# Two reorderings on the tensor engine in batch 0 of an attention and gated-MLP kernel

## The chip, the cores and the metric

The kernel runs on one core of one Trainium2 chip; runs are compared within a job where it can be done. The metric is the device time of one execution in microseconds (us). Engines are written as in the profile: PE is the tensor engine (matmuls), PEld its weight loads, DVE the vector engine, ACT the scalar engine, POOL the GpSimd engine, which issues the loads. In the lines of the profile, 64*128 or 128*128 behind a matmul is the part of the array that it uses, the chain is the sequence of work that ended last, followed back from the end, and "issue" is idle time for which the profile shows no cause.

## The reference

```python
B, H, S, Nb, D = 8, 8, 576, 16, 64
k_all = concatenate([beacon_k, k]);  v_all = concatenate([beacon_v, v])     # 592 keys
scores = q @ k_all.T / sqrt(D), future keys masked with -1e9
a = exp(scores - max);  a /= a.sum() + 1e-9
x = (a @ v_all) as [4608, 512]
# ... [cut: types]
out = (gelu(x @ w_gate) * (x @ w_val)) @ w_out                             # 512 -> 1536 -> 512
```

## The kernel before

Heads are worked in four pairs (0 to 3) per batch. Scores of a pair come in chunks (pair, chunk): matmuls with 64 rows of K, two heads side by side on the two halves of the array, each chunk followed by one exp on ACT. Three PSUM buffers of the pool `psum_s` go round between score chunks, values pairs and gates; `psum_t` and `psum_o` hold one buffer each. In batch 0 the causal mask is added on PE by small matmuls with an identity.

```python
def scores(b, *parts):
    s_ps = psum_s.tile([P, 2, 512], FP32, name="s_ps", tag="s")     # one of three
    # ... score_mms: 64-row matmuls, then the masking matmuls
    act(exp_ring[...], s_ps[...], ACT.Exp, scale=QK_SCALE)
def av(b, m):                       # values of both heads: 30 matmuls, in psum_s
    # ... attend, attend, normalize (reciprocal and product on DVE)
def av_head(b, m, hi, pool, tag):   # one head: 15 matmuls, in psum_t or psum_o
    # ...
def turn(b, m, pool=None, tag="t"): # five PE transposes of the normalised pair
    # ...
def put(b, m, by_act=False):        # copies the turned pair to xT_sb on ACT or DVE
    # ...
```

The order of batch 0's second half, with `c` for `scores(0, ...)`:

```python
c((3, 0)); c((3, 2))
av_head(0, 0, 0, psum_t, "t"); av_head(0, 0, 1, psum_o, "o")
c((2, 3), (3, 3)); av(0, 1); c((3, 1)); av(0, 2)
turn(0, 0); put(0, 0, by_act=True); turn(0, 1, psum_o, "o"); put(0, 1, by_act=True)
av(0, 3); gv_mms(0, 0, 0); turn(0, 2); put(0, 2, by_act=True)
# ... [cut: table load]
gv_mms(0, 1, 0); turn(0, 3, psum_o, "o"); put(0, 3)
for kk in (1, 2, 3):
    for fi in (0, 1):
        gv_mms(0, fi, kk, last=kk == 3)        # gate and value matmuls of row chunk kk
```

The softmax here doesn't subtract the row's maximum and nothing guards it: scores larger than these inputs give would overflow.

## Time and profile before

| what | before |
|---|---|
| time, median of the first three runs | 365.41 us (364.52 to 365.82) |
| profiled span | 363.6 us |
| PE busy | 353.7 us, 97% |
| first weights of (3,0), released by DVE's key copy | 15.87 us |
| first weights of the last turn | 23.71 us |

The prediction shows the lines of the page, the chain of waits and the timeline. The columns are start, length, engine, line, operation, operands and count; in brackets is the idle time before and what ended it.

```profile
19.20 0.11 PEld L168 LDWEIGHTS <-qkT 64*128 64x128 bf16 x4
19.60 0.11 PEld L168 LDWEIGHTS <-eye 64*128 64x128 bf16 x3 [0.29 <-issue]
```

Four weight loads come together at 19.20, and then PE's stream stands for 0.29 us with nothing to wait for that the profile knows ("issue").

### The profile page before, as it was taken

The numbers are of one execution on the slowest core, as the hardware profiler recorded it, in microseconds if no ns is written. First come the engines' busy times: TensorE is split into PE (matmuls) and PEld (weight loads), VectorE is DVE, ScalarE is ACT, GpSimd is POOL, SyncE is SP. The second block draws the span as 40 slices with busy tenths as digits, with TensorE's granted clock in tenths as the row PEclk, the third lists the DMA queues.
The fourth block names the chain that finished last, engine by engine and source line by source line (L and its number), as shares of the span: only waits on it lengthen the run. The fifth ranks groups of instructions, "written<-read, shape, count | busy, mean of one in ns | idle before, by whom it ended". The sixth has DMA issues, their size and how long they took to land.

```text
span 363.6 us, 7732 instructions
## 1 busy us (share of the span) xinstructions
PE 353.7 (97%) x3164; PEld 187.5 (52%) x3206; DVE 163.4 (45%) x320; ACT 193.0 (53%) x252; POOL 161.3 (44%) x288
## 2 busy tenths in 40 slices
PE   7899999999999999999999999999999999999996
PEld 7664546444654455445644564446544554444443
DVE  3548746344453345434534354335443453333322
ACT  3975788237923694358633891379335953321210
POOL 8934387556536552945374545565330530000000
PEclk9999999999999999999999999999999999999999
DMA  8999999899289975999299927993795142000112
GB/s 112 174 203 204 196 121 97 125 156 199 30 128 135 215 58 71 168 217 62 56 138 205 138 38 122 162 198 35 111 147 127 15 65 113 0 2 29 58 38 108
DMA packets 160419, 41.57 MB, mean 114 GB/s; under 512 B 146944, under 2 KB 155904, under 8 KB 160384
## 3 DMA queue, kind: packets, MB, share of 16 engines
q0 software_dynamic: 104848, 19.11, 68.4%
q1 hardware_dynamic: 55536, 21.96, 30.9%
q8 instruction: 25, 0.41, 0.5%
q14 instruction: 10, 0.08, 0.1%
HBM read 38.27 MB, written 9.44 MB: 131 GB/s over the span
## 4 chain that ended last, share of the span: by engine, by line
PE 88%; DMA 5%; DVE 3%; POOL 2%; issue 1%; ACT 0%; SPq 0%; POOLq 0%
PE gv_ps L168 40%; PE o_ps L168 25%; PE x_ps L168 9%; PE s_ps L168 6%; DMA q_sb<-in_q_dram 3%; PE v_ps L168 3%; PE g_ps L168 3%; PE t_ps L176 2%; DMA k_sb<-in_k_dram 1%; DVE qkT L235 1%; POOL v_sb L111 1%; PE w_ps L168 1%; DVE o_sb L481 1%; DMA xT_sb<-y_sb 1%; POOL k_sb L111 0%
## 5 line engine op out<-in xcount | busy, mean ns | idle before, releaser
L171 ACT ACTIVATE ge_sb<-gv_ps 128x512 bf16<-128x512 f32 x95 | 55.8, 597 | 134.7 <-PE gv_ps L168 132.4
L433 DVE TENSOR_TENSOR hT_sb<-gv_ps,ge_sb 128x512 bf16<-128x512 f32 x95 | 64.9, 691 | 105.4 <-ACT ge_sb L171 105.3
L171 ACT ACTIVATE expT<-s_ps 128x992 bf16<-128x992 f32 (+3 forms) x112 | 100.5, 975 | 11.3 <-PE s_ps L168 9.8
L168 PE MATMUL gv_ps<-xT_sb,wg_sb 128*128 128x512 bf16 x378 | 105.1, 379 | 0.5
L168 PE MATMUL o_ps<-wo_sb,hT_sb 128*128 128x512 bf16 (+3 forms) x492 | 101.0, 373 | 2.3 <-DVE o_sb L481 0.9
L168 PE MATMUL gv_ps<-xT_sb,wv_sb 128*128 128x512 bf16 x364 | 101.7, 379 | 0.4
L320 POOL TENSOR_SCALAR_AFFINE_SELECT expT<-expT 128x256 bf16<-128x256 bf16 (+1 forms) x140 | 52.4, 391 | 48.4 <-ACT expT L171 47.1
L168 PEld LDWEIGHTS <-wv_sb 128*128 128x128 bf16 x432 | 42.2, 98 | 50.6
L168 PEld LDWEIGHTS <-wg_sb 128*128 128x128 bf16 x432 | 42.1, 98 | 49.9
L168 PEld LDWEIGHTS <-hT_sb 128*128 128x128 bf16 (+1 forms) x516 | 40.8, 96 | 43.8 <-issue 5.4
L168 PEld LDWEIGHTS <-expT 128*128 128x128 bf16 (+1 forms) x960 | 33.7, 97 | 9.0 <-POOL expT L320 3.1
L168 PE MATMUL x_ps<-v_sb,expT 128*128 128x65 bf16 (+1 forms) x960 | 36.8, 193 | 0.0
L111 POOL DMA_DIRECT2D v_sb<-in_v_dram x40 | 33.7, 861 | 6.1 <-DMA wv_sb<-in_moe_w_val_dram 2.4
L168 PE MATMUL s_ps<-qkT 64*128 64x80 bf16 (+5 forms) x528 | 33.1, 250 | 2.4 <-DVE qkT L239 1.6
L111 POOL DMA_DIRECT2D k_sb<-in_k_dram x30 | 25.2, 843 | 16.8 <-DMA v_sb<-in_v_dram 8.3
L111 POOL DMA_DIRECT2D q_sb<-in_q_dram x30 | 25.3, 874 | 9.9 <-DMA wo_sb<-in_moe_w_out_dram 3.6
L356 DVE TENSOR_TENSOR y_sb<-x_ps,r_sb 128x320 bf16<-128x320 f32 (+1 forms) x47 | 28.8, 612 | 1.8 <-DVE r_sb L354 0.2
L354 DVE RECIPROCAL r_sb<-x_ps 128x5 f32<-128x5 f32 (+1 forms) x47 | 9.6, 204 | 38.9 <-PE x_ps L168 38.9
L479 DVE COPY o_sb<-o_ps 128x512 f32<-128x512 f32 (+2 forms) x31 | 20.7, 668 | 13.3 <-PE o_ps L168 12.7
L168 PEld LDWEIGHTS <-qkT 64*128 64x128 bf16 x528 | 18.6, 95 | 14.0 <-issue 6.1
L399 POOL COPY hold_sb<-xT_sb 128x2 bf16<-128x2 bf16 x6 | 1.1, 186 | 31.9 <-DMA xT_sb<-y_sb 31.9
L433 DVE TENSOR_TENSOR hT_sb<-v_ps,ge_sb 128x512 bf16<-128x512 f32 x13 | 9.0, 692 | 9.5 <-PE v_ps L168 9.5
(58 smaller groups left out, 153.7 us busy)
## 6 DMA issues: line engine op xcount, KB each, us to landing
out_dram<-o_sb SPq DMA_DIRECT2D x35, 256.0 KB, 7.0
v_sb<-in_v_dram POOLq DMA_DIRECT2D x24, 128.0 KB, 9.2
q_sb<-in_q_dram POOLq DMA_DIRECT2D x18, 128.0 KB, 12.8
k_sb<-in_k_dram POOLq DMA_DIRECT2D x18, 128.0 KB, 5.5
wo_sb<-in_moe_w_out_dram POOLq DMA_DIRECT2D x3, 512.0 KB, 14.6
wg_sb<-in_moe_w_gate_dram POOLq DMA_DIRECT2D x2, 512.0 KB, 11.3
wv_sb<-in_moe_w_val_dram POOLq DMA_DIRECT2D x2, 512.0 KB, 13.1
v_sb<-in_v_dram POOLq DMA_DIRECT2D x8, 112.0 KB, 5.7
```

The lines of the kernel that those rows point to most:

```text
L111: keep(nc.gpsimd.dma_start(out=out_ap, in_=in_ap))
L168: keep(nc.tensor.matmul(out_ap, lhsT, rhs, start=start, stop=stop, **kw))
L171: keep(nc.scalar.activation(out_ap, in_ap, func, **kw))
L176: keep(nc.tensor.transpose(out_ap, in_ap, ident[0:n, 0:n]))
L235: keep(nc.vector.tensor_copy(out_ap, in_ap))
L320: nc.gpsimd.affine_select(out=d, in_=d, pattern=[[0, 2], [1, n]], compare_op=ALU.is_ge, fill=0.0, base=0, channel_multiplier=-1,)
L354: keep(nc.vector.reciprocal(r, x[:, :, :, D:DV]))
L356: nc.vector.tensor_tensor(out=y_of[i][:, :, h0:h1, :].rearrange("p j b d -> p b j d"), in0=x[:, :, :, 0:D], in1=r.to_broadcast([P, h1 - h0 ...
L399: keep(nc.gpsimd.tensor_copy(hold_sb, x[:, 0 : S : S - 1]))
L433: keep(nc.vector.tensor_tensor(out=h_of[ci][:, fi, :], in0=v_ps, in1=ge_sb, op=ALU.mult))
L479: keep(nc.vector.tensor_copy(o_ap, o_ps))
L481: keep(nc.vector.tensor_copy(o_ap, o_half))
```

## The change

The first values head of pair 0 is computed one score chunk sooner, while chunk (3,2)'s score buffer is not yet free. The turn of pair 0 goes ahead of values pair 2, so that its copy on ACT follows straight behind the last exp.

```diff
     c((3, 0))
+    av_head(0, 0, 0, psum_t, "t")
     c((3, 2))
-    av_head(0, 0, 0, psum_t, "t")
     av_head(0, 0, 1, psum_o, "o")
     c((2, 3), (3, 3))
     av(0, 1)
     c((3, 1))
+    turn(0, 0)
     av(0, 2)
-    turn(0, 0)
     put(0, 0, by_act=True)
```

## The prediction

> **What bounds the kernel now.** I read the page first (busy shares, then the chain that ended last), then that chain between 12 and 28 us only, and then the timeline of the tensor engine (PE), of its weight loads (PEld), of the scalar engine (ACT) and of the vector engine (DVE) from 14 to 25 us, because the diff touches nothing outside batch 0's values.
>
> ```profile
> PE 353.7 (97%) x3164; PEld 187.5 (52%) x3206; DVE 163.4 (45%) x320; ACT 193.0 (53%) x252; POOL 161.3 (44%) x288
> PE 88%; DMA 5%; DVE 3%; POOL 2%; issue 1%; ACT 0%; SPq 0%; POOLq 0%
> ```
>
> PE is busy for 353.7 of 363.6 us and is 88% of the chain: a change gains only what it takes off PE's sequence, or off a wait in which PE stands still. The chain around the change:
>
> ```profile
> 14.32 1.42 DVE qkT L235 x2
> 15.75 0.08 DVE qkT L239
> 15.83 0.05 issue
> 15.88 0.90 PE s_ps L168 x12
> 16.78 1.02 PE x_ps L168 x30
> ...
> 20.08 1.02 PE x_ps L168 x30
> 21.10 0.53 PE y_ps L176 x10
> 21.63 0.93 PE x_ps L168 x30
> 22.56 0.02 issue
> 22.58 0.23 DVE r_sb L354
> ```
>
> The columns are start, length and what. PE is released at 15.88 us by DVE's copy of the last key tile and from there the chain runs on PE alone, through scores, values and two turns, to the end of the last values pair at 22.56. So both moves lie inside one stretch that PE's own order bounds. Now the single waits in it (start, length, engine, what; in brackets idle time and who ended it):
>
> ```profile
> 16.13 0.28 PEld L168 LDWEIGHTS <-qkT 64*128 64x128 bf16 x2
> 16.32 0.37 PE L168 MATMUL s_ps<-qkT 64*128 64x464 bf16 x2
> 16.52 0.26 PE L168 MATMUL s_ps<-neg,eye 64*128 64x64 bf16 x4
> 16.71 1.09 PE L168 MATMUL x_ps<-v_sb,expT 128*128 128x65 bf16 x30
> 17.73 0.26 PE L168 MATMUL s_ps<-qkT 64*128 64x208 bf16 x2
> ...
> 20.12 1.00 ACT L171 ACTIVATE expT<-s_ps 128x992 bf16<-128x992 f32 x1 [0.45 <-PE s_ps L168]
> 21.40 1.19 ACT L171 ACTIVATE xT_sb<-y_ps 128x576 bf16<-128x576 bf16 x2 [0.28 <-PE y_ps L176]
> 23.28 0.65 ACT L171 ACTIVATE xT_sb<-y_ps 128x576 bf16<-128x576 bf16 x1 [0.69 <-PE y_ps L176]
> 23.71 0.28 PEld L176 LDWEIGHTS <-y_sb 128*128 128x128 bf16 x5 [0.54 <-DVE y_sb L356]
> ```
>
> The reader is to see three things. Score chunk (3,2) has its first weights at 16.13, but its matmul starts only at 16.32. ACT waits 0.28 us for the turned pair 0, the wait that the second move aims at. And the only long stop of PE's sequence after 15.88 is the last turn, which waits for the normalised fourth pair, not for anything that is moved.
>
> **What the Trainium skill says.** TensorEngine Tiling (Array Packing), Tiling Modes, Key Properties: changing the tiling mode, not just the tile, drains the TensorE. Scores run here as 64*128 tiles, values as 128*128, so each change between them should cost. The trace agrees: the four small masking matmuls before another score take 0.08 to 0.09 us to the next start (14.80 to 14.89, 17.83 to 17.91), but 0.19 and 0.18 us before values (16.52 to 16.71, 18.00 to 18.18): 0.10 us for scores to values. Thirty values matmuls take 0.92 to 0.93 us when a turn or a gate matmul, also 128*128, follows (20.01 to 20.94, 21.46 to 22.38), but 1.02 when a score follows (16.71 to 17.73, 18.18 to 19.20): 0.095 us for the way back. Perfetto Trace Analysis, Per-instruction lifecycle, Tensor Engine Instruction: the profiler estimates a matmul's end. I therefore work with starts throughout. TensorE: Matmul & The Clock Gate, Single matmul latency: (398 + N)/2.4 ns warm, which for N = 80 is 0.20 us (an estimate from that page); the exp at 20.12 follows the last masking matmul, start about 19.89, by 0.23 us, so it roughly agrees.
>
> **Part one, the first values head (15 matmuls) goes ahead of chunk (3,2).** No instruction is added or removed; the listing of the two programs' orders differs on PE alone, and each engine has the same number of rows.
> Removed: a wait. Chunk (3,2) needs the score buffer of (2,2), one of three, whose exp runs from 15.28 for 0.94 us, to 16.22. PE is through with (3,0) at about 16.10 + 0.09 = 16.19, and (3,2) starts at 16.32: 0.13 us of standing. In the new order the head fills it, being in another buffer: -0.13 us.
> Can the head start then? Its exps, pair 0's, are long over. The values land about 6 us after their issues, which start from 6.99 to about 10.5: the last at some 16.0 to 16.5, and the head needs the last tile in its fifteenth matmul only, at about 16.75. I take it as no wait.
> Added: scores and values alternate once more. Before: (3,0) (3,2) | head 0, head 1 | (2,3)(3,3). After: (3,0) | head 0 | (3,2) | head 1 | (2,3)(3,3). One more change in each direction is 0.10 + 0.095 = +0.195 us.
> Step by step: (3,0) done 16.19; head 0 from 16.29 with 15 x 0.031 = 0.46 to 16.75; (3,2) from 16.85 for 0.20 + 0.09 = 0.29 to 17.13; head 1 from 17.23 to 17.69; (2,3)(3,3) at 17.79, where it is 17.73 today. Sum +0.195 - 0.13 = **+0.06 us** on PE.
> Does the later (3,2), 0.5 us, starve ACT? Exp (3,0) starts at 16.98 and exp (3,2) about 17.9. The scores are ready at about 17.13 + 0.2 = 17.3: 0.6 us to spare, no cost. The head's normalisation comes 0.5 us earlier on DVE, which had been idle for 1.56 us there; nothing on PE waits for it: the next user of that result is the turn, three microseconds later.
>
> **Part two, turn (0,0) ahead of values pair 2.** The turn is five transposes in 0.26 us (ten from 20.94 to 21.46). Pair 0 is normalised at 18.23 + 0.49 = 18.72, so it can run at 20.0 without a wait. PE's sum up to the end of pair 3 stays: the same 2 x 30 values matmuls and 10 transposes, all 128*128, so no further mode change. 0.0 us on PE.
> What moves: the copy of pair 0 on ACT need not wait for the turn, only for the last exp, which ends at 21.12: it starts at about 21.15 to 21.2 instead of 21.40, and the second copy ends at about 22.4 instead of 22.59. The first gate matmul needs the first copy, which today ends at 22.05, and starts at 22.38 because PE comes free then; the second copy is first needed at 23.95. Both had over 0.3 us of slack already. ACT's gain of 0.2 us is off the path: worth 0.
> Given back: pair 2 ends 0.26 us later, and its normalised result goes from 22.21 to about 22.5 (with the 0.06 of part one). Turn (0,2) loads it at 22.60 today, at about 22.66 then: just in time, 0.1 us of slack left.
> The end of the stage is pair 3's end, plus reciprocal and product on DVE (22.58 to 23.66), plus the last turn at 23.71. All shift by the +0.06.
>
> **Sum.** 365.41 + 0.06 = 365.47; I write 365.45, since half of such a sum can vanish in rounding of the starts. From 24 us on PE runs without a break, so it is carried to the end unless the chain's DMA share (5%) takes it in.
>
> **Rivals.** (a) The mode change is cheaper for a short run, and the removed wait stands: -0.13 to 0 us, 365.3. For: only four places are measured. Against: all four agree within 0.02 us. (b) The transfers bite: if the last values tile lands later than estimated, head 0 now stops in front of (3,2), up to 0.3 us, 365.75; for it speaks the estimate's half microsecond of doubt, against it that today's head at 16.71 shows no stop. (c) Turn (0,2) becomes the stop: if DVE is 0.1 us later than worked out, PE waits some 0.1 us, but the last turn waits for DVE anyway (0.54 us on the loads' row), and DVE's product for pair 3 is only late if the one before is; 365.45 to 365.55. (d) The intent comes true, copies earlier mean gates earlier, worth the 0.28 us of ACT's wait: 365.15. Against it: PE, not the copies, sets the first gate's start.
>
> **Range and chances.** All of these lie between -0.3 and +0.35 us, 0.1% of the span, below the spread of the three runs before (364.52 to 365.82, 1.3 us). So the range is set by that spread: 364.6 to 366.2. 2% would be 7.3 us, nearly the whole 8.3 us from 15.88 to 24.16 in which the change lies: within 2% has 0.98, the rest split evenly.
>
> **What would show it right or wrong.** Right: 15 values matmuls start at about 16.3, (3,2) near 16.85, two more gaps of 0.1 us; chunk (2,3)(3,3) starts 0.06 us later counted from the end of DVE's key copy; ACT's first copy waits for the exp instead of the turn and starts 0.2 us sooner; the last turn still waits for DVE. Wrong: a stop inside head 0 (b), a stop before turn (0,2) (c), the last turn more than 0.1 us sooner from the key copy (a, d), or a difference of over 0.5 us that arises after 25 us, where no instruction moved.

## The result

| | before | changed |
|---|---|---|
| first comparison, median of 6 runs each | 365.51 us (364.52 to 365.82) | 365.02 us (364.92 to 365.40) |
| ratio, 95% interval | | 0.9993 [0.9981, 1.0006] |
| second comparison (nine runs of before, five of the changed, below) | 364.83 us (364.40 to 365.59) | 365.08 us (364.32 to 365.21) |
| ratio, 95% interval | | 1.0003 [0.9988, 1.0017] |

A ratio is the mean time of one kernel's runs over that of the other's runs of the same rounds, so it is not quite the ratio of the medians. The first comparison has the changed kernel a little ahead, the second a little behind.

The page of the changed kernel, busy times and chain by engine:

```profile
PE 356.0 (98%) x3206; PEld 187.7 (52%) x3206; DVE 163.6 (45%) x320; ACT 193.0 (53%) x252; POOL 161.6 (44%) x288
...
PE 96%; DVE 3%; issue 0%; ACT 0%
```

PE's 356.0 us against 353.7 is no added work: the count of matmul records is 3206 against 3164, so 42 were missing from the trace before. The 5% of DMA in the chain before are gone as well. With its records complete, the chain runs through PE and DVE alone, and so does that of the kernel before in its second trace, which has all 3206 records too. So I read that share as most likely an effect of missing records, and not as time that transfers bound; it is not quite shown, for two other complete traces keep 1 and 2% of DMA in the chain.

The chain of the changed kernel around the change (start, length, what):

```profile
14.46 1.42 DVE qkT L235 x2
15.88 0.09 DVE qkT L239
15.97 0.05 issue
16.02 0.47 PE s_ps L168 x6
16.49 0.56 PE x_ps L168 x15
17.05 0.39 PE s_ps L168 x6
17.44 0.56 PE x_ps L168 x15
18.00 0.46 PE s_ps L168 x12
```

The whole stage starts 0.14 us later than in the trace before, because the key copy came later. Where before the chain had twelve score matmuls and then thirty values matmuls, it now alternates six, fifteen, six, fifteen, which is the new order. The single instructions, from the timeline:

```profile
16.42 0.63 PE L168 MATMUL x_ps<-v_sb,expT 128*128 128x65 bf16 x15
...
16.99 0.37 PE L168 MATMUL s_ps<-qkT 64*128 64x464 bf16 x2
...
17.37 0.63 PE L168 MATMUL x_ps<-v_sb,expT 128*128 128x65 bf16 x15
...
17.93 0.26 PE L168 MATMUL s_ps<-qkT 64*128 64x208 bf16 x2
...
19.40 0.11 PEld L168 LDWEIGHTS <-qkT 64*128 64x128 bf16 x4
...
19.63 0.11 PEld L168 LDWEIGHTS <-eye 64*128 64x128 bf16 x3
...
20.15 1.00 ACT L171 ACTIVATE expT<-s_ps 128x992 bf16<-128x992 f32 x1 [0.34 <-PE s_ps L168]
...
21.04 1.30 ACT L171 ACTIVATE xT_sb<-y_ps 128x576 bf16<-128x576 bf16 x2
...
22.63 0.48 PEld L176 LDWEIGHTS <-y_sb 128*128 128x128 bf16 x5
...
23.74 0.28 PEld L176 LDWEIGHTS <-y_sb 128*128 128x128 bf16 x5 [0.54 <-DVE y_sb L356]
```

The prediction's times were worked out for a key copy as in the trace before. Put 0.14 us later, they are 16.43, 16.99, 17.37 and 17.93: four starts, each met within 0.01 us. ACT's first copy of a turned pair has lost its bracket: it waits for no turn any more. Yet the last turn comes at 23.74, that is 7.73 us after (3,0), not 7.84 + 0.06 = 7.90. The difference arises in chunk (3,1), between the loads at 19.40 and at 19.63: they are 0.23 us apart, where before they were 0.40 apart.

### The profile page after: what moved, and what is told of

The parts are those of the page before. It is cut to its first block, busy times and chain, and to the rows that moved or that the text cites. A ratio compares the mean times of both kernels' runs of the same rounds, so it can differ in the third digit from the quotient of the medians.

```text
span 363.6 us, 7774 instructions
## 1 busy us (share of the span) xinstructions
PE 356.0 (98%) x3206; PEld 187.7 (52%) x3206; DVE 163.6 (45%) x320; ACT 193.0 (53%) x252; POOL 161.6 (44%) x288
## 4 chain that ended last, share of the span: by engine, by line
PE 96%; DVE 3%; issue 0%; ACT 0%
PE gv_ps L168 45%; PE o_ps L168 26%; PE x_ps L168 9%; PE s_ps L168 7%; PE v_ps L168 3%; PE g_ps L168 3%; PE t_ps L176 2%; DVE qkT L235 1%; DVE o_sb L481 1%; PE w_ps L168 1%; PE y_ps L176 0%; ACT qkT L171 0%; DVE o_sb L479 0%; DVE qkT L239 0%; DVE idle L80 0%
## 5 line engine op out<-in xcount | busy, mean ns | idle before, releaser
L168 PE MATMUL o_ps<-wo_sb,hT_sb 128*128 128x512 bf16 (+3 forms) x516 | 104.8, 373 | 0.9 <-DVE o_sb L481 0.9
L168 PE MATMUL gv_ps<-xT_sb,wv_sb 128*128 128x512 bf16 x380 | 105.3, 379 | 0.0
```

Of the source, the lines that this page charges most:

```text
L168: keep(nc.tensor.matmul(out_ap, lhsT, rhs, start=start, stop=stop, **kw))
```

## The experiments

All distances below are counted on weight loads from the first one of chunk (3,0), to take the arrival of the inputs out of them. Chunk (3,1) takes 0.47 us from its first load to that of the next stage in every trace without a stop; what it takes beyond is called the stop's excess. A wait inside the values heads is taken as the gap there beyond that of the same place in the first trace of the changed kernel (0.15 us from a head's last load to the next score), or beyond 0.03 us between two values loads.

### What varies by itself: both kernels once more

> The kernel before, unchanged, profiled once more, to see what varies by itself. All distances are counted on the weight loads from the first one of score chunk (3,0), which DVE's last key copy releases. In the first trace of before: chunk (2,3)(3,3) at 1.86 us, chunk (3,1) at 3.33 us, a stop of 0.40 us inside (3,1) between its first weights and its first masking weights (0.17 us where chunk (2,1) does the same), first gate at 6.48 us, last turn at 7.84 us. In the trace of after: 1.92, 3.39, stop 0.23, 6.37, 7.73. Theory A (the order sets the stop in (3,1): PE's array is behind its instruction stream by more in the new order, so a pause of the stream inside (3,1) is covered): the stop is 0.40 again, last turn 7.84 within 0.03. Theory B (the stop is chance, DMA or instruction fetch): it differs by 0.1 us or more here, and so does the last turn.

> The changed kernel once more. Theory A: stop in (3,1) 0.23 us within 0.03, last turn 7.73 us after (3,0)'s first weights. Theory B: the stop is anywhere from 0.17 to 0.40, the last turn from 7.67 to 7.90.

There is no edit. The kernel before took 365.11 us, the changed one 365.27. The stop in (3,1), from the timeline of the repeated kernel before:

```profile
18.67 0.11 PEld L168 LDWEIGHTS <-qkT 64*128 64x128 bf16 x4
19.38 0.11 PEld L168 LDWEIGHTS <-eye 64*128 64x128 bf16 x3 [0.59 <-issue]
```

and of the repeated changed kernel:

```profile
19.49 0.11 PEld L168 LDWEIGHTS <-qkT 64*128 64x128 bf16 x4
19.53 0.25 PEld L168 LDWEIGHTS <-eye 64*128 64x128 bf16 x4
```

The same program has an excess of 0.34 us in one execution and 0.65 in another; the changed one has 0.17 and none. Theory A, by which the order sets the stop, falls. Theory B, chance, stands. From the last turn to the program's last weight load these four traces, and the two of the next section, took 336.50 to 336.53 us. So what these executions differ in lies before the last turn.

### Each half alone

`e1_head_only` against the kernel before:

```diff
+    av_head(0, 0, 0, psum_t, "t")
     c((3, 2))
-    av_head(0, 0, 0, psum_t, "t")
```

> Only the first values head moves ahead of chunk (3,2); turn (0,0) stays behind values pair 2. The ledger of the prediction (two mode changes of 0.1 us in, a 0.13 us buffer wait out): (2,3)(3,3) at 1.92 us, and all after it 0.06 later than in before: last turn at 7.90. Theory A: (2,3)(3,3) at 1.92 too, but the stop in (3,1) shrinks to about 0.23 us and the last turn is at 7.73: the gain of 0.11 us comes from this part alone. ACT's first copy still waits for the turn in both.

`e2_turn_only` against the kernel before:

```diff
+    turn(0, 0)
     av(0, 2)
-    turn(0, 0)
```

> Only turn (0,0) goes ahead of values pair 2. The ledger and theory A agree: nothing on PE up to (3,1), stop there 0.40 us, first gate at 6.48, last turn at 7.84 us; ACT's first copy starts 0.2 to 0.3 us sooner relative to the last exp and earns nothing. A rival (earlier copies start the gates earlier): first gate at 6.2 and last turn at 7.6 us.

They took 364.83 and 364.70 us (one run each). With the head alone, (2,3)(3,3) starts at 1.92 us; with the turn alone, at 1.85, as before. The last turn came at 7.80 and 7.49 us, with an excess of 0.24 and none in (3,1): 7.56 and 7.49 without it. So the 0.06 us belongs to the head and nothing to the turn. Read raw, the turn alone seems to bear out its rival (first gate at 6.13 us, last turn at 7.49, where 6.2 and 7.6 were named), but it is the missing stop that does this: less the excess, the first gate is at 6.13 in before as well, and at 6.20 in the changed kernel and with the head alone. On ACT, the timeline with the head alone:

```profile
19.60 1.00 ACT L171 ACTIVATE expT<-s_ps 128x992 bf16<-128x992 f32 x1 [0.41 <-PE s_ps L168]
20.88 1.19 ACT L171 ACTIVATE xT_sb<-y_ps 128x576 bf16<-128x576 bf16 x2 [0.28 <-PE y_ps L176]
```

The wait of 0.28 us for the turn is there as before; in the changed kernel it is gone. The copy starts 1.28 us after the last exp's start here and in before, and 0.89 us after it in the changed kernel: 0.39 us sooner, and PE does not profit.

### The ledger of waits

| trace | (2,3)(3,3) at | wait in the heads | excess in (3,1) | last turn at | less both |
|---|---|---|---|---|---|
| before | 1.85 | 0 | 0.34 | 7.84 | 7.50 |
| before, again | 1.79 | 0 | 0.65 | 8.09 | 7.44 |
| turn only | 1.85 | 0 | 0 | 7.49 | 7.49 |
| changed | 1.92 | 0 | 0.17 | 7.73 | 7.56 |
| changed, again | 1.97 | 0.05 | 0 | 7.61 | 7.56 |
| head only | 1.92 | 0 | 0.24 | 7.80 | 7.56 |
| changed, timed | 1.92 | 0 | 0.15 | 7.70 | 7.55 |
| changed, 74 warm-ups | 2.18 | 0.26 | 0 | 7.82 | 7.56 |
| changed, 70 warm-ups | 1.92 | 0 | 0 | 7.56 | 7.56 |

The last column is 7.55 to 7.56 us in all six traces with the early head. Without it, it is 7.44 to 7.50, the 7.44 where the buffer wait ahead of (3,2) happened to be 0.06 us shorter.

### More alternation or less: both heads ahead of (3,2)

`e4_both_heads` against the changed kernel:

```diff
     av_head(0, 0, 0, psum_t, "t")
+    av_head(0, 0, 1, psum_o, "o")
     c((3, 2))
-    av_head(0, 0, 1, psum_o, "o")
```

> The changed kernel with the second values head of pair 0 ahead of chunk (3,2) too: the buffer wait stays filled, and scores and values change as often as in before. Ledger: after (3,0) 0.41 us, 30 values matmuls 0.93, change 0.095, (3,2) 0.28: (2,3)(3,3) at 1.72 us, where before has 1.86 and the change 1.92; stage to the last turn, less the excess of a stop in (3,1), 7.36 us against 7.50 (before) and 7.56 (changed). Rival: the mode changes are not what costs, the 0.06 us came from the head itself: (2,3)(3,3) at 1.85 to 1.92 and the stage at 7.5 to 7.6. Danger: ACT gets (3,2) 0.1 us too late; then exp (3,2) waits, and PE not.

It took 365.05 us (one run). Its weight loads:

```profile
15.99 0.51 PEld L168 LDWEIGHTS <-expT 128*128 128x128 bf16 x15
16.72 0.52 PEld L168 LDWEIGHTS <-expT 128*128 128x128 bf16 x15 [0.23 <-issue]
17.29 0.10 PEld L168 LDWEIGHTS <-qkT 64*128 64x128 bf16 x2
```

Thirty values loads should follow each other at 0.03 us, but after the fifteenth comes a gap of 0.32 us. The fifteenth matmul is the one that waits for the last values tile, so this is rival (b) of the prediction, with an excess of 0.29 us. The trace has the landing too: that tile lands at 16.68 us and the fifteenth matmul starts at 16.72. (2,3)(3,3) starts at 1.95, less 0.29 at 1.66; the last turn at 7.63, less 0.29 at 7.34. Expected were 1.72 and 7.36. (The 1.66 is early because the weights are loaded ahead where a score precedes; the first matmul of the chunk comes at 2.01, less 0.29 at 1.72.) Taking one pair of mode changes out is worth 7.56 - 7.34 = 0.22 us (0.195 expected). The rival, that the head itself costs, falls.

In this trace the gain did not reach the end of the program. From the last turn to the last weight load it took 336.72 us, 0.2 more than the six before, and the difference arises in batch 1, where PE waits for a masking on POOL:

```profile
52.72 0.36 PE L168 MATMUL x_ps<-v_sb,expT 128*128 128x65 bf16 x6 [0.29 <-POOL expT L320]
```

Whether the new order brings this wait or chance does, one trace cannot tell. The run with both steps together, below, has PE there as early and no such wait.

### The wait of the last turn

`e5_gate_fill` against the changed kernel:

```diff
     gv_mms(0, 1, 0)
+    for fi in (0, 1):
+        gv_mms(0, fi, 1)
     turn(0, 3, psum_o, "o")
     put(0, 3)
-    for kk in (1, 2, 3):
+    for kk in (2, 3):
```

> The changed kernel with the four gate and value matmuls of the second row chunk ahead of the last turn, where PE waits 0.54 us by its loads for DVE's product. If that wait is PE's real loss (I count 0.2 us of matmul time that stands still), the wait is gone and the first matmul of the third row chunk starts about 0.2 us sooner, 8.44 us after (3,0) less the stop's excess, against 8.65 in the changed kernel. If the wait moves to the last row chunk, which needs the copy of the last turn, nothing is gained: 8.65 or later at the last chunk.

It took 364.90 us (one run). The last turn's loads, which had waited for DVE for 0.54 us in every kernel so far, from its timeline:

```profile
23.85 0.48 PEld L176 LDWEIGHTS <-y_sb 128*128 128x128 bf16 x5
```

There is no wait. Compared at one weight load of the last row chunk that both orders have in the same place: 9.64 us after (3,0) here and 9.52 in the changed kernel. Less the heads' wait of 0.51 us here and the excess of 0.17 there, it is 9.13 against 9.35: 0.22 us sooner, 0.2 expected. The heads' wait hides it in this execution:

```profile
15.74 0.36 PEld L168 LDWEIGHTS <-expT 128*128 128x128 bf16 x10
16.29 0.21 PEld L168 LDWEIGHTS <-expT 128*128 128x128 bf16 x5 [0.18 <-issue]
16.82 0.10 PEld L168 LDWEIGHTS <-qkT 64*128 64x128 bf16 x2 [0.32 <-issue]
```

The tenth and the fifteenth matmul of a head are the first users of the last two values tiles. These land at 16.24 and 16.66 us, and the two matmuls start at 16.28 and 16.70. At 53.6 us, in batch 1, this trace too loses about 0.1 us.

### Both steps together, timed

`e6_both_fill` has both edits.

> Both steps together: both heads ahead of (3,2), gates of the second row chunk ahead of the last turn. The ledger sums to -0.14 - 0.20 = -0.34 us against before (365.4 to 365.5), so 365.1, ratio 0.999; in the trace the third row chunk 8.24 us after (3,0), less the stop's excess. Rest of the program from there as constant as in all traces so far (336.50 to 336.53 us from the last turn to the last weight load). If the sum is not additive because DVE or ACT becomes the bound once PE is quicker, 8.3 to 8.6.

It took 364.92 us, median of five, against 365.19: ratio 0.9996 [0.9982, 1.0010]. In its trace the same load of the last row chunk comes at 9.61 us, less the excess of 0.61 in (3,1) at 8.99; in before at 9.63 less 0.34, 9.29. That is about 0.3 us sooner, 0.34 expected. The timeline shows where 0.08 us went back: values pair 1, whose loads span 0.96 us in the other kernels, takes

```profile
17.61 1.04 PEld L168 LDWEIGHTS <-expT 128*128 128x128 bf16 x30
```

with one gap, after its first load. This pair reuses the score buffer of (3,0), by the order of the allocations, and that chunk's exp ends at 17.65 us, 0.05 before the pair's first matmul at 17.70. (Chunk (3,2) in before follows the exp of its buffer by the same 0.05 us.) A plain gain in the stage, then, but the timing cannot tell it from nothing. I do not call this version faster.

### Where the stop in (3,1) comes from

`e3_fewer_warm` against the kernel before, and `e7_warm74` and `e8_warm70` against the changed one, differ in one number:

```diff
-    warm(66)
+    warm(50)    # e3; 74 in e7, 70 in e8
```

> The kernel before with 50 warm-up matmuls for 66, so every later PE instruction stands 32 places earlier in PE's stream. Runs so far: a stop of 0.18 to 0.69 us in chunk (3,1), always right after the same 352nd weight load, in four traces of six; none in two. If the stop belongs to a place in the stream (fetch of PE's instructions), it now comes 16 weight loads later in the program, at the start of values pair 2 behind (3,1), or not at all, and (3,1) takes its plain 0.47 us. If it belongs to what (3,1) does (its buffer, its operands), it is again behind the fourth weight load of (3,1) in most traces. Stage from (3,0) to the last turn without the stop: 7.50 us as in before; the warm-up itself should cost nothing, as PE waits for keys after it.

> The changed kernel with 74 warm-up matmuls for 66: everything later on PE stands 16 instructions (8 weight loads) later in PE's stream. So far the stop came in 5 of 9 traces with 66 warm-ups, always after the 352nd weight load, which is the fourth of chunk (3,1); with 50 warm-ups it came in neither place. If it belongs to the place in the stream, it comes now, if at all, eight loads earlier in the program, at the end of values pair 1, and (3,1) takes its plain 0.47 us. If it belongs to (3,1), it is again after that chunk's fourth load. PE may start the key transposes some 0.3 us later, as the warm-up ends later than the keys land.

> The same with 70 warm-ups: the 352nd weight load is now the last but one of values pair 1's, just ahead of (3,1). Stream theory: a stop, if it comes, directly ahead of (3,1)'s first load or before; theory of (3,1) itself: after its fourth load, as before.

None of the three has a stop, in (3,1) or at the shifted place, so by their own test they settle nothing: with a stop in six of the ten traces that have 66 warm-ups, three misses can be chance. What settles more is a record that I had overlooked, the transfers of the instruction queue. There are 25 of 16 KB each in a run. The second one, in the DMA view of the kernel before for 17.2 to 17.3 us (packets, MB, share):

```profile
q8 instruction: 1, 0.02, 60.9%
```

I took its end in all thirteen traces and set it against the weight load at which PE resumes, the one behind the 352nd. In the six traces with a stop, PE resumes 1.30 to 1.48 us after the transfer's end, whether the stop lasted 0.19 or 0.69 us from load to load. In the seven without, PE reaches that load later than that, 2.0 to 4.4 us after the end in six of them and 1.42 us in one, which was just in time. In every trace with 66 warm-ups the fourth transfer starts when PE is at load 481, 129 loads and so some 258 instructions behind the 352nd. So I read the stop as a boundary of PE's instruction stream, which PE can cross only some 1.3 to 1.5 us after an instruction transfer has ended; its length is set by when that transfer ended. (The profile does not say whose instructions a transfer carries.) The Trainium skill, Runtime: NRT & Kernel Launch, Instruction fetch mechanics, has streams refilled in 16 KiB blocks of 256 instructions, with a cost at a boundary that it calls "mostly hidden". The size agrees; here the cost was in the open for 0.15 to 0.65 us. No run delayed an instruction transfer on purpose, and no shifted stop was caught, so the cause is well supported and not proven.

These runs told two more things. `e7_warm74` took 365.58 us, and its chain shows rival (b) in the open:

```profile
11.39 0.28 issue
11.68 5.53 DMA v_sb<-in_v_dram
17.21 0.04 issue
17.25 0.19 PE x_ps L168
```

The last values tile was issued late there (11.68 us against 10.43 in before) and landed at 17.21, and the first head waited for it. `e8_warm70` took 366.59 us although its stage is the shortest of the changed order (7.56, no wait at all). It lost 1.2 us far behind the change:

```profile
183.93 0.10 PEld L168 LDWEIGHTS <-wg_sb 128*128 128x128 bf16 x1
185.34 0.10 PEld L168 LDWEIGHTS <-wv_sb 128*128 128x128 bf16 x1 [1.31 <-issue]
```

That is a stop of the same kind, "issue", at a place where no other trace has one. Here too an instruction transfer ends just before, at 184.01 us, and PE goes on 1.33 us after it, within the 1.30 to 1.48 of the stops in (3,1). One look at a time would have told a wrong story in either case.

`e3_fewer_warm` took 367.22 us against 365.19 and does not carry its own "should cost nothing". Its matmuls, from the timeline:

```profile
7.68 0.61 PE L168 MATMUL s_ps<-qkT 64*128 64x512 bf16 x2 [0.75 <-ACT qkT L171]
...
15.28 0.63 PE L168 MATMUL s_ps<-qkT 64*128 64x512 bf16 x2
...
18.22 0.39 PE L168 MATMUL s_ps<-qkT 64*128 64x512 bf16 x2 [0.46 <-DVE qkT L239]
```

The same pair takes 0.61 to 0.63 us until some 16 us and 0.39 after; in before it takes 0.39 already at 7.66. The granted clock of the profile does not show this. It reads 1.00, as in this row of the windows view (stretch, its length, busy time of PE, PEld, DVE, ACT and POOL, granted clock, DMA share, GB/s):

```profile
12.00:16.00 4.00, 4.00 (x66) 2.75 (x62) 1.50 (x3) 3.17 (x5) 3.65 (x5) 1.00 2.14 169
```

Fifty warm-ups fill 2.85 us; the 66 of before fill 3.70. The Trainium skill, TensorE: Matmul & The Clock Gate, What's actually happening, says that PE's clock is released after about 3.4 us of sustained work; these two numbers lie on either side of that. The trace of before is slower to release than 3.4 us, though: its first twelve transposes, from 4.76 to 5.45 us, still take 0.69 us as in this run. That the shorter warm-up is the cause is therefore likely, from one execution. The run also shows the buffer wait by contrast: PE comes so late here that (3,2) finds its buffer free, and starts 0.31 us after (3,0) instead of 0.45 (18.22 to 18.53, against 15.87 to 16.32). Its stage is 7.35 us, where the expectation had 7.50: the buffer wait is missing here.

### The changed kernel timed again

> The changed kernel timed in five rounds against the one before. The ledger says +0.06 us, the chance terms (start of the last key tile 15.34 to 16.04 us, stop in (3,1) 0 to 0.65 us, values landing 0 to 0.5 us) spread single runs by about 1 us: ratio 1.000 with an interval of about plus or minus 0.001. A real gain of 0.26 us, as the first medians had it, would be 0.9993 again. In this trace: stage from (3,0) to the last turn, less the stop and less stops inside head 0, 7.56 us.

There is no edit. The median is 365.08 us against 364.83, ratio 1.0003 [0.9988, 1.0017]; the stage without stops is 7.55 us. The lead of the first comparison did not come again.

## Why the prediction was right

**The time.** 365.45 was predicted, with 364.6 to 366.2; 365.02 was measured. The middle was 0.43 us high. The range came from the spread of the runs, so a forecast of no change would have hit it as well; the time alone says nothing for the sum of +0.06 us. One median of six does not know it better than to some tenths: the second comparison, in a later job, moved the kernel before by 0.7 us, from 365.51 to 364.83.

**Part one, the sum.** The +0.06 us was right in size and in parts: the four starts of the changed stage were met within 0.01 us, the head alone brings it (7.56 against 7.49 and 7.50 us), and the turn brings nothing. The two terms were tested apart. The buffer wait is absent where PE comes late (0.31 against 0.45 us, so about 0.13). A pair of mode changes less is worth 0.22 us, where 0.195 was reckoned. Two slips did no harm: the exp that frees (3,2)'s buffer ends at 16.27 us and not at 16.22 (it takes 0.99 us), and the latency formula, which its page gives for a full 128-row matmul, was put to N = 80 where the last masking matmul has N = 64. Neither enters the sum.

**"I take it as no wait".** This step was half right, and that the first trace had no wait was partly luck. A head stopped for values in four of the nine traces with the early head (the changed kernel again 0.05 us, 74 warm-ups 0.26, both heads 0.29, gates ahead of the turn 0.51), and not at all in the other five, among them the first trace of the change. Rival (b) deserved more weight: the early head hangs on a transfer whose landing varies.

**Part two.** Right that it earns nothing. ACT's gain was 0.39 us instead of 0.2, in part because the copy's record starts before the exp's ends (21.04 against 20.15 + 1.00). Turn (0,2) did fit: its loads at 22.63 carry no wait, so rival (c) falls, and (d) falls since the gates did not move with the copies (first gate, less the excess, at 6.13 us both in before and with the turn alone). Rival (a) falls with the starts.

**What was missed.** The prediction said that a last turn more than 0.1 us sooner would show it wrong. The first trace had exactly that, 7.73 against 7.84 us, and the sum was right all the same. The missing term was the stop in (3,1), which stood in the profile before as 0.29 us of "issue". I took it as a fixed part of the stage, but its excess varies from 0 to 0.65 us. "The only long stop of PE's sequence after 15.88 is the last turn" was the step that failed. Also, "it is carried to the end" held in the traces of the change, except where a stop of 1.2 us came with 70 warm-ups, but in the one trace with both heads ahead 0.2 us went back to a wait for POOL in batch 1. The DMA share of the chain, with which I hedged, came most likely from missing records.

## What to carry to other kernels

Count the changes between 64-row and 128-row matmuls when reordering: filling a wait of 0.13 us with work of the other kind cost 0.2 us in changes here and lost. For effects of a tenth, compare stages in several traces from a common releasing event, and take stops named "issue" and transfer waits out first; a pair of traces, or a pair of medians, told the wrong sign here. Removing an idle time on an engine beside the critical one, ACT's 0.28 us, earned nothing here. And follow a gain in one stage to the end of the program: in one trace here 0.2 us of it went back in the next batch.

## What the Trainium skill lacked or had wrong

- TensorEngine Tiling (Array Packing) says that changing the tiling mode drains the array, without a price. Here one change each way between 64*128 and 128*128 cost about 0.2 us (0.195 from the trace before, 0.22 by taking a pair out).
- Runtime: NRT & Kernel Launch calls the cost at an instruction block's boundary mostly hidden. If the stop in (3,1) is such a boundary, as argued above, it was not: PE stood 0.15 to 0.65 us beyond its plain time in six of ten traces, and resumed 1.30 to 1.48 us after the end of an instruction transfer.
- TensorE: Matmul & The Clock Gate gives the time that releases the clock. It does not say how long a kernel with short pauses can stay slow once it has missed it: here, in the one run with 50 warm-ups, until about 16 us, and the run took 2.0 us more in all.
